# Pair loads, later weights, a new order of the scores and masks on another engine in a fused attention and mixing kernel

## The chip, the cores and the metric

One core of a Trainium2 chip. The metric is the device time of one execution in microseconds (us). Most executions of one kernel lie within a few us of one another. Engines are named as in the profile: PE (matrix products), DVE (vector), ACT (scalar), POOL (general purpose), SP (issues most of the DMAs).

A ratio between two kernels is the mean time of one kernel's fast runs over that of the other's in the same rounds. It is not quite the ratio of the medians quoted beside it.

## The reference

Eight batches, eight heads, 576 tokens, head size 64, all float32.

```python
q_d, k_d, v_d = mean of q, k, v over groups of 4 tokens           # 144 pooled tokens
out_up    = repeat(softmax(q_d @ k_d.T / 8) @ v_d, 4)             # pooled attention
out_local = softmax(q @ k.T / 8 where |i - j| < 4) @ v            # banded attention
x     = heads of (out_up + out_local) side by side                # (8, 576, 512)
theta = x @ w_theta
y     = w_tok_r @ (x * cos(theta)) + w_tok_i @ (x * sin(theta))   # over tokens
u     = x + y
out   = u + relu(u @ w_ch)
```

## The kernel before

Three generators make the work of a batch: `attention` (to x), `modulate` (theta, z) and `mix` (y and the output). A period runs attention of batch b+1, modulate of b and mix of b-1, interleaved by a fixed list. Attention 0 runs by itself, then the two token matrices are turned by PE, then the periods start. "First period" below is attention 1 with modulate 0; it has no mix. The parts that the change touches:

```python
TR = 96; NTR = S // TR                      # tokens of q, k in 6 tiles of 96
def load_qk(b):                             # 64 floats = 256 bytes in one piece
    for nm, src in (("q", q), ("k", k)):
        for c in range(6): nc.sync.dma_start(out=t[:, c, :, :],
            in_=src[b, :, TR*c:TR*c+TR, :].rearrange("h p d -> p h d"))
# [... load_v likewise; casts to bf16: batch 0 on DVE (q), POOL (k), ACT (v), later ones on POOL ...]
nc.gpsimd.dma_start(out=wth, in_=moe_w_theta ...)        # theta as bf16, software queue
for ri, w_dram in enumerate((moe_w_tok_r, moe_w_tok_i)): # token matrices, channel weights too
    nc.gpsimd.dma_start(out=t[:, 0:4, :], in_=w_dram[0:512, :] ...)
# [...]
def attention(b):
    # [... pstr: q, k turned and pooled by one product with ip = (identity | pooling);
    #      ACT copies the tokens to qT, kT, DVE the pooled ones to qdT, kdT; psvd: pooled v;
    #      psSd: pooled scores, exps on ACT to pd ...]
    for c in range(5):                                   # banded scores, exps, masks
        # [... psS products into a large PSUM tile, two of which exist (tag "w2") ...]
        nc.scalar.activation(out=pm[...], in_=ps[...], func=AF.Exp, scale=SCL)
        nc.gpsimd.affine_select(out=pm[...], in_=pm[...], ...)   # lower edge of the band
        nc.gpsimd.affine_select(out=pm[...], in_=pm[...], ...)   # upper edge
    for g in range(2):                                   # pooled output: psnd, also in "w2"
        # [... 16 products; rd = 1 / sum; xd = psnd * rd, both on DVE ...]
    for c in range(5):
        # [... psup (xd spread to tokens), psloc (pm @ v); rl, tmp, x on DVE ...]
# [... modulate, mix ...]
drain(attention(0)); drain(build_WT())                   # turning stands alone
for b in range(B + 1):
    run(attention(b + 1), modulate(b), mix(b - 1))       # with ends of the range cut
```

The softmax here doesn't subtract the row's maximum and nothing guards it: scores larger than these inputs give would overflow.

## Time and profile before

| | before |
|---|---|
| time of the runs beside the changed kernel | 360.19 us median of 4 (358.78 to 360.47) |
| profiled span, mean granted PE clock of the view | 358.8 us, 0.955 |
| last v cast of batch 0 ends | 38.48 us |
| last x of attention 0 ends | 56.24 us |
| first xTps (modulate 0 starts) | 62.29 us |
| psSd of batch 1 (pooled scores of the first period) | 75.49 us |
| first psth of the second period | 96.75 us |
| full periods at clock 1.0 | 36.06 us |

These landmarks are starts or ends of single instructions in the order of time. Two of them bracket the start of the program: up to the last v cast it waits for data, and from the first psth of the second period on every period looks alike. The prediction shows lines of the order of time (columns: start, duration, engine, source line, operation, output and inputs with sizes, count, and in brackets the idle time before it with what ended it).

```profile
86.48 0.69 DVE L319 TENSOR_TENSOR xd<-psnd,rd 72x512 bf16<-72x512 f32 x1
86.53 2.13 POOL L295 TENSOR_SCALAR_AFFINE_SELECT pm<-pm 128x1024 bf16<-128x1024 bf16 x2
...
88.52 0.69 DVE L355 TENSOR_TENSOR tmp<-psloc,rl 120x512 bf16<-120x512 f32 x1
...
92.94 0.87 POOL L298 TENSOR_SCALAR_AFFINE_SELECT pm<-pm 100x768 bf16<-100x768 bf16 x1
...
94.76 0.20 DVE L353 RECIPROCAL rl<-psloc 96x8 f32<-96x8 f32 x1 [1.18 <-PE psloc L346]
...
96.35 0.67 DVE L362 TENSOR_TENSOR x<-tmp,psup 96x512 bf16<-96x512 bf16 x1
```

POOL masks until 93.8. But DVE's rl, tmp and x start at 88.3 beside it and end at 97.0, and in these 8.7 us DVE waits only twice, 0.36 and 1.18 us.

A caution on the clock. A profile holds records of it only from its first rise on, at 67.2 us here and at 54.8 in the changed kernel, and the views count time without a record as 1.0. The products say otherwise. Two equal groups of the changed kernel, one before its first record and one after:

```profile
49.86 1.91 PE L484 MATMUL psth<-wth,xT 128*120 128x512 bf16 x4
...
55.18 1.03 PE L484 MATMUL psth<-wth,xT 128*120 128x512 bf16 x4
```

In all twenty profiles the products that turn q and k (pstr) follow one another every 120 ns (100 in the kernel before) both up to the first record and where half is recorded, and every 62 ns (52) where 1.0 is recorded. So up to the first record every kernel ran at half clock, and the clock that a view gives for a stretch ahead of the first record, or for one that reaches into it, is too high (the prediction's 0.73 over 62 to 96 us is some 0.65).

### The profile page before, as it was taken

The page shows a single profiled execution, that of the slowest core. Times are in us where ns is not written, and L with a number is a line of the kernel's source. Part 1 is how long each engine was busy: PE and PEld are TensorE (multiplying, and loading weights), DVE is VectorE, ACT ScalarE, POOL GpSimd, SP SyncE. Part 2 cuts the span into 40 slices and gives each one's busy share as a digit, 9 for nine tenths or more (in the row PEclk, how much of TensorE's full clock was granted, in tenths as well). Part 3 has the DMA queues.
Part 4 walks back from the last instruction along what each step waited for, and adds up shares of the span by engine and source line. Part 5 has one row for each costly group of instructions (what it writes and reads, how often), then busy time and mean ns, then how long its engine had stood idle before and what let it go on. Part 6 is the DMA issues. An engine that isn't in the chain of part 4 may idle for free.

```text
span 358.8 us, 7037 instructions
## 1 busy us (share of the span) xinstructions
PE 296.6 (83%) x2834; PEld 201.8 (56%) x2834; DVE 193.5 (54%) x435; ACT 192.1 (54%) x283; POOL 156.2 (44%) x153
## 2 busy tenths in 40 slices
PE   0025689948799989999899989998999899979995
PEld 0023368526566656665666666656665676657672
DVE  1121076533754494629574876287628752865433
ACT  1024802585267735782669366936693679334303
POOL 8011396308831783377147817583458003700000
PEclk9999999985589998999899999999999999999999
DMA  8999989990291069936994499766001200210303
GB/s 151 200 187 198 181 154 156 193 178 14 48 200 27 5 180 173 195 53 175 179 195 79 117 218 174 118 145 153 0 3 62 74 0 3 81 53 2 117 16 132
DMA packets 122577, 41.18 MB, mean 115 GB/s; under 512 B 115760, under 2 KB 117936, under 8 KB 122544
## 3 DMA queue, kind: packets, MB, share of 16 engines
q1 hardware_dynamic: 120272, 38.35, 55.2%
q0 software_dynamic: 2272, 2.38, 4.0%
q8 instruction: 22, 0.36, 0.4%
q14 instruction: 11, 0.09, 0.1%
HBM read 33.65 MB, written 9.44 MB: 120 GB/s over the span
## 4 chain that ended last, share of the span: by engine, by line
PE 47%; DVE 20%; ACT 15%; SPq 7%; issue 4%; POOL 3%; DMA 3%; POOLq 0%; ACTq 0%
PE psu L421 18%; PE psth L396 9%; SPq L80 6%; PE psr L439 6%; DVE osb L451 4%; DVE tmp L355 4%; DVE z L405 4%; DVE x L362 4%; PE pstr L212 3%; ACT pd L259 3%; PE psS L282 3%; ACT L259 2%; PE psnd L311 2%; PE wps L187 2%; ACT vd L240 2%
## 5 line engine op out<-in xcount | busy, mean ns | idle before, releaser
L421 PE MATMUL psu<-WT,z 120*128 120x288 bf16 (+1 forms) x640 | 93.6, 292 | 2.5 <-DVE uT L430 2.5
L421 PEld LDWEIGHTS <-z 120*128 120x128 bf16 (+1 forms) x640 | 60.5, 100 | 23.2 <-issue 3.6
L295 POOL TENSOR_SCALAR_AFFINE_SELECT pm<-pm 128x1024 bf16<-128x1024 bf16 (+1 forms) x40 | 41.2, 1047 | 65.5 <-ACT pm L289 65.5
L449 ACT ACTIVATE rel<-psr 128x512 f32<-128x512 f32 (+1 forms) x40 | 23.8, 596 | 61.7 <-PE psr L439 61.7
L430 DVE TENSOR_TENSOR uT<-psu,xT 128x288 bf16<-128x288 f32 x64 | 26.8, 452 | 50.7 <-PE psu L421 50.7
L396 PE MATMUL psth<-wth,xT 128*120 128x512 bf16 (+1 forms) x160 | 45.1, 406 | 7.6 <-DVE xT L386 6.8
L405 DVE TENSOR_TENSOR z<-cs,x 120x1024 bf16<-120x1024 bf16 (+1 forms) x40 | 39.1, 977 | 17.4 <-ACT cs L404 17.3
L219 ACT CAST qT<-pstr 128x576 bf16<-128x576 f32 x32 | 20.3, 640 | 52.1 <-PE pstr L212 52.1
L403 ACT ACTIVATE cs<-psth,pihc 120x512 bf16<-120x512 f32 (+1 forms) x40 | 27.5, 687 | 35.8 <-PE psth L396 35.6
L106 POOL CAST k_tm<-k 96x1536 bf16<-96x1536 f32 x16 | 24.5, 1547 | 41.6 <-DMA k<-in_k_dram 17.5
L439 PE MATMUL psr<-wch,uT 128*128 128x512 bf16 (+1 forms) x160 | 42.1, 379 | 0.0
L298 POOL TENSOR_SCALAR_AFFINE_SELECT pm<-pm 128x1024 bf16<-128x1024 bf16 (+1 forms) x40 | 41.1, 1047 | 0.3
L106 POOL CAST q_tm<-q 96x1536 bf16<-96x1536 f32 x14 | 23.2, 1679 | 40.5 <-PE pstr L212 32.2
L212 PE MATMUL pstr<-ip,q_tm 96*128 96x120 bf16 x192 | 19.8, 249 | 21.8 <-DVE ip L129 11.8
L289 ACT ACTIVATE pm<-psS 128x1024 bf16<-128x1024 f32 (+1 forms) x40 | 36.4, 981 | 1.9 <-PE psS L282 1.5
L451 DVE TENSOR_TENSOR osb<-rel,psx 128x512 f32<-128x512 f32 (+1 forms) x40 | 27.3, 682 | 7.9 <-ACT rel L449 7.1
L396 PEld LDWEIGHTS <-xT 128*120 128x120 bf16 (+1 forms) x160 | 20.5, 139 | 17.3 <-DVE xT L386 8.1
L212 PEld LDWEIGHTS <-q_tm 96*128 96x128 bf16 x192 | 14.6, 115 | 26.5 <-DVE ip L129 11.8
L386 DVE COPY xT<-xTps 128x480 bf16<-128x480 bf16 (+1 forms) x40 | 15.5, 389 | 25.7 <-PE xTps L381 25.6
L355 DVE TENSOR_TENSOR tmp<-psloc,rl 120x512 bf16<-120x512 f32 (+1 forms) x40 | 26.9, 685 | 0.1
L362 DVE TENSOR_TENSOR x<-tmp,psup 120x512 bf16<-120x512 bf16 (+1 forms) x40 | 26.5, 675 | 0.0
L346 PEld LDWEIGHTS <-pm 128*128 128x128 bf16 (+1 forms) x320 | 17.2, 113 | 15.9 <-issue 7.3
(68 smaller groups left out, 417.6 us busy)
## 6 DMA issues: line engine op xcount, KB each, us to landing
q<-in_q_dram SPq DMA_DIRECT2D x48, 192.0 KB, 5.6
k<-in_k_dram SPq DMA_DIRECT2D x48, 192.0 KB, 4.9
v<-in_v_dram SPq DMA_DIRECT2D x32, 256.0 KB, 5.3
out_dram<-osb SPq DMA_DIRECT2D x32, 256.0 KB, 2.0
v<-in_v_dram SPq DMA_DIRECT2D x8, 200.0 KB
out_dram<-osb SPq DMA_DIRECT2D x8, 128.0 KB
wtm<-in_moe_w_tok_r_dram POOLq DMA_DIRECT2D x1, 576.0 KB, 9.3
wtm<-in_moe_w_tok_i_dram POOLq DMA_DIRECT2D x1, 576.0 KB, 12.0
```

What stands on the lines that cost most here:

```text
L106: eng(out=dst[:, 3 * i:3 * i + 3], in_=src[:, 3 * i:3 * i + 3])
L212: nc.tensor.matmul(out=ps[:, c // 3, (c % 3) * TW:(c % 3) * TW + TW], lhsT=tm[:, c, 2 * hh:2 * hh + 2, :], rhs=ip, start=True, stop=True,)
L289: nc.scalar.activation(out=pm[0:kw, :, 0:qn], in_=ps[0:kw].rearrange("p e (j w) -> p (e j) w", w=P)[:, :, 0:qn], func=AF.Exp, scale=SCL,)
L295: nc.gpsimd.affine_select(out=pm[0:kw, :, 0:qn], in_=pm[0:kw, :, 0:qn], compare_op=ALU.is_ge, fill=0.0, base=off, pattern=[[0, 8], [-1, qn ...
L298: nc.gpsimd.affine_select(out=pm[0:kw, :, 0:qn], in_=pm[0:kw, :, 0:qn], compare_op=ALU.is_ge, fill=0.0, base=6 - off, pattern=[[0, 8], [1, ...
L355: nc.vector.tensor_tensor(out=tmp[0:cnt].rearrange("p (j e d) -> p e j d", e=2, j=4), in0=pv[0:cnt, :, :, 0:D], in1=rl[0:cnt].unsqueeze(3) ...
L362: nc.vector.tensor_tensor(out=x[0:cnt], in0=tmp[0:cnt], in1=up[0:cnt], op=ALU.add)
L396: nc.tensor.matmul(out=th[0:cnt, :], lhsT=xT[:, dc, QS[c]:QS[c] + cnt], rhs=wth[:, dc, :], start=(dc == 0), stop=(dc == 3),)
L405: nc.vector.tensor_tensor(out=z[0:cnt, c, :, :], in0=cs[0:cnt], in1=xt[c][0:cnt].unsqueeze(1).to_broadcast([cnt, 2, DM]), op=ALU.mult,)
L421: nc.tensor.matmul(out=pss[hf][:, 0:288], lhsT=z[0:QC[c], c, ri, P * dc:P * dc + P], rhs=WT[0:QC[c], ri, c, 288 * hf:288 * hf + 288], star ...
L439: nc.tensor.matmul(out=psr[0:cnt, :], lhsT=uT[:, dc, OS[c]:OS[c] + cnt], rhs=wch[:, dc, :], start=(dc == 0), stop=(dc == 3),)
L451: nc.vector.tensor_tensor(out=osb[0:cnt], in0=rel[0:cnt], in1=psx[0:cnt, 0:DM], op=ALU.add)
```

## The change

The intent: the start waits for data, and DMA is full there with pieces of 256 bytes. So q and k are loaded as pairs of tokens (512 bytes), q by head. Theta comes as float32 by the hardware queue, the other weights are asked for inside the first period, and the turning of the token matrices goes into that period too. POOL's masks at the start move to DVE as one product with a band. The pooled output moves ahead of most banded scores. The pair layout costs an interleaving write on ACT. Two small savings: five psvd products instead of six, and the last output block as 128 x 256 instead of 64 x 512.

```diff
-                        in_=src[b, :, TR * c:TR * c + TR, :].rearrange("h p d -> p h d"),
+                        in_=src[b, h].rearrange("(c p r) d -> p c (r d)", c=NTR, r=2),        # q, by head
+                    in_=src[b, :, TB * c:TB * c + TB, :].rearrange("h (p r) d -> p h (r d)", r=2),   # k
-    nc.gpsimd.dma_start(out=wth, in_=moe_w_theta.rearrange("(c p) e -> p c e", p=P))
+    nc.sync.dma_start(out=w32, in_=moe_w_theta.rearrange("(c p) e -> p c e", p=P))   # cast by POOL
-    w_tm = [] ... nc.gpsimd.dma_start(...)          # token matrices, wch outside
     def build_WT():
+        w_tm = [] ... nc.gpsimd.dma_start(...)      # now inside
-                    in_=pv[:, :, :, 0:TR],
+                    out=To[:, hh, :].rearrange("p (c w r) -> p c r w", c=NTR, r=2),   # ACT, interleaving
-        for g, cs in ((0, (0, 1, 2)), (1, (2, 3, 4))):
+        for g, cs in ((0, (0, 1, 2)), (1, (3, 4))):
+            if b == 0 or (b == 1 and c % 2 == 0):
+                nc.vector.tensor_tensor(out=pv, in0=pv, in1=band[min(c, 1)]..., op=ALU.mult)
+            else: nc.gpsimd.affine_select(...) twice, as before
-        for c in range(NCH): scores; then for g in range(2): pooled output
+        scores(0); pooled_out(0); scores(1); pooled_out(1); scores(2); scores(3); scores(4)
-    drain(build_WT())
-            mix(b - 1) if b >= 1 else None)
+            mix(b - 1) if b >= 1 else build_WT())
# [... cut: constants, casts in thirds with a pace, last output block, buffers of v_w and vd kept ...]
```

## The prediction

> **What bounds the kernel now.** I read the row of slices first, then a table of busy time by stage, then the order of time of the first 65 us, then the chain that ended last inside one full period, then the groups and the DMA queues.
>
> ```profile
> PE   0025689948799989999899989998999899979995
> POOL 8011396308831783377147817583458003700000
> PEclk9999999985589998999899999999999999999999
> DMA  8999989990291069936994499766001200210303
> ```
>
> A slice is 9 us. The DMA engines are full for the first nine slices while PE is empty for two and partly filled until slice 10; POOL is full where PE's clock falls (slices 8 to 10). From slice 11 on PE is at 9 tenths. So there is a start of some 96 us that PE does not bound, and a steady part that PE nearly does. The table by stage gives sizes (columns: window, length, busy us and count on PE, PEld, DVE, ACT, POOL, granted clock, DMA share, GB/s):
>
> ```profile
> 12.00:30.00 18.00, 3.48 (x30) 2.57 (x27) 2.19 (x5) 2.42 (x4) 2.91 (x2) 1.00 1.09 194
> 54.00:62.00 8.00, 8.00 (x56) 6.40 (x54) 5.67 (x13) 2.56 (x3) 5.74 (x6) 1.00 1.04 157
> 62.00:96.20 34.20, 24.92 (x234) 17.22 (x233) 17.22 (x41) 18.33 (x28) 17.17 (x16) 0.73 0.65 105
> 135.00:172.70 37.70, 35.20 (x348) 23.45 (x348) 23.13 (x53) 23.70 (x36) 19.30 (x17) 0.95 0.73 150
> 210.60:246.60 36.00, 33.51 (x348) 22.55 (x348) 23.20 (x53) 23.68 (x36) 21.38 (x18) 1.00 0.85 164
> ```
>
> The first 30 us hold 4 us of PE work: attention of batch 0 waits for data. 54 to 62 is the turning of the two token matrices, alone. 62 to 96 is the first overlapped period, without mix, yet as long as a full one. Full periods last 36.0 at full clock, up to 38.8 where it drops.
>
> The order of time shows the waits of the start:
>
> ```profile
> 10.66 0.96 DVE L106 CAST q_tm<-q 96x1536 bf16<-96x1536 f32 x1 [8.00 <-DMA q<-in_q_dram]
> 19.46 0.96 DVE L106 CAST q_tm<-q 96x1536 bf16<-96x1536 f32 x1 [7.74 <-DMA q<-in_q_dram]
> 28.55 1.46 POOL L106 CAST k_tm<-k 96x1536 bf16<-96x1536 f32 x1 [1.76 <-DMA k<-in_k_dram]
> 37.87 0.61 ACT L111 CAST v_w<-v 100x512 bf16<-100x512 f32 x1
> 43.62 2.13 POOL L298 TENSOR_SCALAR_AFFINE_SELECT pm<-pm 128x1024 bf16<-128x1024 bf16 x2
> 56.16 0.81 DVE L192 COPY WT<-wps 120x576 bf16<-120x576 bf16 x2
> 62.29 0.98 PE L381 MATMUL xTps<-ident,x 120*128 120x120 bf16 x8
> ```
>
> q is complete at 19.5, k at 28.6, v at 37.9; then POOL masks five score blocks, two passes of 1.07 each, to 53; then the turning; modulate of batch 0 begins at 62.3. In the period after it the chain is
>
> ```profile
> 81.27 1.03 ACT pm L289
> 82.36 2.13 POOL pm L295 x2
> 84.50 2.09 POOL pm L298 x2
> 86.58 2.09 POOL pm L295 x2
> ```
>
> POOL to 93.8, with PE idle and its clock halved. In a full period (135 to 173) the chain is PE to the second psr, then some 10 us of DVE (osb, tmp, x in turn) to the next xT. The DMA side:
>
> ```profile
> q1 hardware_dynamic: 120272, 38.35, 55.2%
> q0 software_dynamic: 2272, 2.38, 4.0%
> ```
>
> **What the Trainium skill says.** "DMA: Bandwidth & Descriptors", section Specifications, puts the least transfer for full rate at 512 B; its section on small descriptors adds a fixed overhead per packet. The trace agrees in kind: 115760 of 122577 packets are under 512 B and saturated stretches move 154 to 200 GB/s. "TensorE: Matmul & The Clock Gate", Part 1, says that an idle window of about 3.4 us halves the clock: the trace has 0.73 over 62 to 96. "VectorE: DVE Perf Modes", tier table, gives tensor_tensor on bf16 in SBUF two elements a cycle; the like-shaped z product takes 0.68 us undisturbed (0.93 on average), so a mask product should cost 0.65 to 0.95 instead of POOL's 2 x 1.09. "TensorE", Part 3, says that products with outputs in different column groups run side by side; no row of this trace shows that yet.
>
> **The change, part by part.**
>
> *DMA.* The hardware queue took 0.552 x 16 x 358.8 = 3169 us of engine time for 120272 packets. Taking 75 ns for each of the 4608 output packets of 2 KB (estimate from 27 GB/s per engine, the page's Specifications), the 256 B ones take 24.4 ns. For 512 B I add 256 B at that rate, 9.4 ns: 34 ns, an estimate. Per batch, over 16 engines: q or k 4608 x 24.4 = 7.0 us before, 2304 x 34 = 4.9 after; v 4896 x 24.4 = 7.5 in both. The software queue's weights took 4.0% = 14.4 us: each token matrix 3.8, each square one 3.4; theta as float32 on the hardware queue 512 x 75 = 2.4. The busy share stood near 1.1 when saturated, so I divide sums by 1.1 and start at 2 us.
>
> The instruction order shows a catch: the first token matrix's load is not a period later at all; it is POOL's first instruction. The second and the channel weights do wait, behind v's casts. So: first token matrix and q0 land at 2 + 8.7/1.1 = 10, k0 at 14.4, v0 at 21.2; then theta, second token matrix, channel weights and q1 (14.5) at 34, k1 at 39, v1 at 46.
>
> *Attention 0.* q cast 12; but the pooling half of ip is behind the first k cast on POOL (13). Four q groups took 3.6 us, so 16.6. PE then meets a psvd product between the first and second k group, which needs v's first cast; POOL does 4.6 us of constants first, so that cast ends near 21. k groups to 25, last v cast 25, pooled exps 26 to 28.7, five banded exps of 0.98 to 34, masks on DVE right behind. DVE then has five tmp, x and rl of 1.5 each: first x at 36, last at 41.5. So modulate 0 starts at 36 against 62.3: 26 us gained, 12 from data that comes earlier, 7 from the masks, and the rest from the turning that no longer stands alone.
>
> *First period.* In before, xTps to vd took 14.3 us (ACT and PE mixed), so vd at 51.5 with 1 us for q copies that were done ahead before; inputs are there (v1 at 46, cast 48). Table load and pooled exps to 57, banded exps to 62. Three of five masks are on DVE; blocks 1 and 3 stay on POOL, behind casts of batch 2 (q2 50, k2 55, v2's first part 58), so they end near 61 and 65. x done 67, first psth 67 against 96.95: the period takes 31 to 32 instead of 34.7, though it holds the turning (50 products, 5.9 to 8 us PE; 4.5 us DVE), since POOL's 11 us of masks are gone from its chain. Gain so far 30.
>
> *Full periods.* psvd is five products of 512 columns instead of six: -0.21. The last output block is 128 x 256 instead of 64 x 512: DVE 0.67 to about 0.4, ACT 0.59 to 0.38, PE 0 to -0.4. The pooled product and its rd/xd go ahead of the scores, but PE's sum ahead of the second psr stays and the chain did not wait for xd. POOL casts 9 pieces of about 1.03 instead of 7 (+0.4), off the path. So -0.5 a period, six periods -3; the last two stages -0.5 each. Total 360.3 - 30 - 3 - 1 = 326.
>
> **Rivals.** (1) *Transfers hidden anyway:* if the start were bound by latency and not by DMA time, loads by pairs would give little. Against: share 0.98 to 1.28 until 54 us, and waits on q and k stand at the head of three casts. It would leave only masks and turning, some 343. (2) *POOL or v take the wait's place:* psvd early in PE's order, and casts of batch 2 ahead of batch 1's masks, make v0 and v2 the gate. I count part of it; if SWDGE packets crowd out q0 as they did at 6 to 23 us, where the second half of q took 9 us longer than the first, all slips by 5 to 8: 332 to 334. (3) *Strided ACT writes:* q and k are written two elements apart now; if 0.64 became 1.1, ACT gains 4 us a period and a period might lengthen by 1 to 2: 335. ACT's 24 us of 36 speak for slack. (4) *Clock:* three boundaries in before lost 1.7 each; the shorter period may meet the idle windows none or five times: +-5.
>
> **Range and chances.** Lengths of the start are good to 5 us each way, the clock to 5, the periods to 3: 317 to 336. For less than 2% (above 353) the whole start would have to fail. Faster 0.97, same 0.02, slower 0.01.
>
> **What would show it.** q_tm casts near 10, last k cast near 15, last v cast near 25; first xTps near 36; first period's POOL masks ending near 65; psth of the second period near 67; full periods of 35.3 to 35.6 at clock 1.0; relu and osb of the last block near 0.4. Wrong would be: q landing after 14, qT copies over 0.7, a PE wait on v_w of several us beyond 21, or periods no shorter than 36.

## The result

| | before | after | predicted |
|---|---|---|---|
| time, median of 4 | 360.19 us | 346.18 us (342.45 to 347.6) | 326 (317 to 336) |
| ratio of fast runs | 1 | 0.9584, 95% interval 0.9503 to 0.9666 | |
| last v cast of batch 0 ends | 38.48 | 28.76 | 25 |
| last x of attention 0 ends | 56.24 | 50.01 | 41.5 |
| first xTps | 62.29 | 45.92 | 36 |
| psSd of batch 1 (the prediction is for vd, which began at 76.50 and 63.28) | 75.49 | 62.16 | 51.5 |
| first psth of the second period | 96.75 | 85.75 | 67 |
| from there to the last period's first psth | 221.4 | 218.5 | about 218.4 |
| from there to the end | 40.7 | 41.7 | about 39.7 |

The changed kernel is faster by some 4%, and 20 us slower than predicted, outside the range. The profiled execution was the slowest of its four (347.6, marked slow for being 1.5% above the fastest); every reading below is repeated in fast profiles of the experiments. Rows of its page and its hardware queue:

```profile
PE   0148889898999889998999899979998999889994
PEclk9999999755899989998999999999999999989999
DMA  8989989967089374618354564520003000300303
...
q1 hardware_dynamic: 84448, 39.40, 47.3%
```

A slice is 8.6 us. PE fills up two slices earlier than before, and DMA's full stretch is shorter: the queue took 47.3% instead of 55.2%. But PE's clock still falls, in slices 7 to 10 (up to 54.8 us, in slice 6, it has no record and was at half), and the boundary that stood at slice 11 has only moved to slice 10. The order of time of the start:

```profile
13.15 1.89 DVE L134 CAST q_tm<-q 96x1024 bf16<-96x1024 f32 x3 [9.53 <-DMA k<-in_k_dram]
...
18.96 1.03 POOL L134 CAST k_tm<-k 96x1024 bf16<-96x1024 f32 x1 [1.05 <-DMA k<-in_k_dram]
...
25.19 0.58 PE L297 MATMUL psvd<-v_w,pu 128*90 128x512 bf16 x1 [3.88 <-POOL v_w L137]
...
28.14 0.62 POOL L141 CAST v_w<-v 100x512 bf16<-100x512 f32 x1
...
36.60 1.17 PE L384 MATMUL psnd<-vd,pd 90*72 90x65 bf16 x16 [0.92 <-DVE xd L392]
36.85 1.53 DVE L363 TENSOR_TENSOR pm<-pm,band 128x1024 bf16<-128x1024 bf16 x1 [0.30 <-POOL q_tm L134]
...
45.92 0.56 PE L469 MATMUL xTps<-ident,x 120*128 120x120 bf16 x4
```

(The releaser named for the q cast is the load that landed last by the profile.) q and k are complete at 15 and 20 instead of 20.4 and 30, v at 28.8 instead of 38.5. PE stands 3.9 us for v's first cast, which POOL makes behind 4 us of constants. A pooled output waits for DVE, and a mask takes 1.53 us where 0.65 to 0.95 was expected. The table by stage, first for the first period and then for two full ones (columns as in the prediction's table):

```profile
45.92:85.75 39.83, 36.03 (x305) 24.84 (x304) 27.64 (x60) 23.12 (x32) 18.60 (x17) 0.74 0.95 196
85.75:122.89 37.14, 34.75 (x350) 23.67 (x352) 22.30 (x51) 25.00 (x36) 22.16 (x21) 0.96 0.57 138
197.42:233.02 35.60, 33.11 (x349) 22.83 (x351) 21.86 (x51) 24.64 (x36) 20.12 (x19) 1.00 0.52 132
```

The first period got longer: 39.83 from first xTps to the next first psth, against 34.46. PE is busy for 36 of it, at a clock of 0.74 by the view, or some 0.63 if the 8.9 us without a record count as half. Full periods at clock 1.0 are 35.60, as predicted. So all of the shortfall lies ahead of 85.75 us, but for the tail, which lost 1.0 instead of gaining 1 (a fall of the clock, see below). The last output block came as foreseen: its osb 410 ns and its relu 384. And its products in two column groups do run side by side, as the prediction expected: the two of a pair start 3 to 30 ns apart, and pair follows pair after 0.11 us.

### The profile page after: what moved, and what is told of

Its sections match the earlier page's. It is cut to its first block, busy times and chain, and to the rows that moved or that the text cites. A ratio compares the mean times of both kernels' runs of the same rounds, so it can differ in the third digit from the quotient of the medians.

```text
span 345.9 us, 7082 instructions
## 1 busy us (share of the span) xinstructions
PE 296.1 (86%) x2844; PEld 203.2 (59%) x2858; DVE 193.0 (56%) x440; ACT 198.1 (57%) x280; POOL 152.5 (44%) x162
## 3 DMA queue, kind: packets, MB, share of 16 engines
q1 hardware_dynamic: 84448, 39.40, 47.3%
## 4 chain that ended last, share of the span: by engine, by line
PE 47%; DVE 19%; ACT 19%; issue 5%; DMA 4%; SPq 3%; POOL 2%; ACTq 0%; DVEq 0%
PE psu L509 17%; PE psth L484 12%; DVE tmp L442 5%; DVE x L449 5%; PE pstr L272 5%; DVE osb L556 4%; PE psnd L384 4%; ACT pm L357 3%; ACT pd L323 3%; DMA k<-in_k_dram 2%; ACT L323 2%; ACT cs L491 2%; ACT rel L554 2%; PE psr L529 2%; PE psS L349 2%
## 5 line engine op out<-in xcount | busy, mean ns | idle before, releaser
L509 PE MATMUL psu<-WT,z 120*128 120x288 bf16 (+1 forms) x640 | 91.3, 291 | 0.0
L370 POOL TENSOR_SCALAR_AFFINE_SELECT pm<-pm 128x1024 bf16<-128x1024 bf16 (+1 forms) x32 | 33.8, 1064 | 48.8 <-ACT pm L357 48.8
L357 ACT ACTIVATE pm<-psS 128x1024 bf16<-128x1024 f32 (+1 forms) x40 | 38.5, 982 | 20.7 <-PE psS L349 14.2
L554 ACT ACTIVATE rel<-psr 128x512 f32<-128x512 f32 (+1 forms) x40 | 22.4, 559 | 48.0 <-PE psr L529 37.7
L280 ACT CAST qT<-pstr 128x576 bf16<-128x576 f32 x32 | 25.5, 802 | 42.1 <-PE pstr L272 42.1
L134 POOL CAST q_tm<-q 96x1024 bf16<-96x1024 f32 x21 | 27.0, 1321 | 47.9 <-PE pstr L272 38.1
L134 POOL CAST k_tm<-k 96x1024 bf16<-96x1024 f32 x24 | 27.6, 1176 | 41.9 <-DMA k<-in_k_dram 16.2
L493 DVE TENSOR_TENSOR z<-cs,x 120x1024 bf16<-120x1024 bf16 (+1 forms) x40 | 31.4, 786 | 17.5 <-ACT cs L492 17.5
L491 ACT ACTIVATE cs<-psth,pihc 120x512 bf16<-120x512 f32 (+1 forms) x40 | 27.5, 688 | 23.8 <-PE psth L484 23.4
L272 PE MATMUL pstr<-ip,q_tm 96*128 96x144 bf16 x192 | 21.5, 264 | 18.4 <-POOL ip L161 16.2
L372 POOL TENSOR_SCALAR_AFFINE_SELECT pm<-pm 128x1024 bf16<-128x1024 bf16 (+1 forms) x32 | 33.4, 1053 | 1.0
L529 PE MATMUL psr<-wch,uT 128*128 128x512 bf16 x114 | 31.3, 379 | 1.4 <-issue 0.8
L272 PEld LDWEIGHTS <-q_tm 96*128 96x128 bf16 x192 | 17.1, 116 | 23.0 <-DVE ip L163 16.0
L484 PEld LDWEIGHTS <-xT 128*120 128x120 bf16 (+1 forms) x160 | 20.4, 141 | 16.0 <-DVE xT L474 6.8
L280 ACT CAST kT<-pstr 128x576 bf16<-128x576 f32 x32 | 24.9, 809 | 6.4 <-PE pstr L272 6.4
L449 DVE TENSOR_TENSOR x<-tmp,psup 120x512 bf16<-120x512 bf16 (+1 forms) x40 | 26.8, 681 | 0.0
```

The lines of the kernel that those rows point to most:

```text
L134: eng(out=dst[:, c].rearrange("p r h d -> p h r d"), in_=src[:, c].rearrange("p h (r d) -> p h r d", r=2))
L272: nc.tensor.matmul(out=ps[:, c, TR * r:TR * r + TR + TP], lhsT=tm[:, c, r, 2 * hh:2 * hh + 2, :], rhs=ip[:, TR * r:TR * r + TR + TP], star ...
L280: nc.scalar.copy(out=To[:, hh, :].rearrange("p (c w r) -> p c r w", c=NTR, r=2), in_=bass.AP(tensor=parts.tensor, offset=parts.offset, ap= ...
L357: nc.scalar.activation(out=pv, in_=ps[0:kw].rearrange("p e (j w) -> p (e j) w", w=P)[:, :, 0:qn], func=AF.Exp, scale=SCL,)
L370: nc.gpsimd.affine_select(out=pv, in_=pv, compare_op=ALU.is_ge, fill=0.0, base=off, pattern=[[0, 8], [-1, qn]], channel_multiplier=1)
L449: nc.vector.tensor_tensor(out=x[0:cnt], in0=tmp[0:cnt], in1=up[0:cnt], op=ALU.add)
```

## The experiments

All edits are against the changed kernel unless said otherwise. Eighteen kernels ran; all gave a result that passed the comparison. The runs of one group shared a chip and the runs of the kernel before (median 360.64, 359.02, 359.01, 360.32 and 359.36 us in the five groups, in the order of this section save where noted). Landmarks in us from each profile:

| run | time, median (range) | ratio to before | last v cast | first xTps | psSd of batch 1 | second period's first psth | full period at clock 1.0 |
|---|---|---|---|---|---|---|---|
| e1_scores_first | 342.34 (341.82 to 343.96) | 0.9526 | 26.79 | 44.97 | 60.62 | 83.30 | 35.42 |
| e2_masks_pool | 347.44 (346.0 to 349.17) | 0.9662 | 27.65 | 43.77 | 66.35 | 87.40 | 35.59 |
| e3_both | 343.24 (342.96 to 343.63) | 0.9544 | 27.43 | 42.94 | 61.98 | 83.41 | 35.42 |
| e4_turn_alone | 349.93 (347.57 to 351.86) | 0.9720 | 27.35 | 55.70 | 67.50 | 89.14 | 35.60 |
| e7_const_first | 340.42 (338.24 to 344.15) | 0.9515 | 25.16 | 40.72 | 55.41 | 78.72 | 35.59 |
| e8_late | 336.81 (333.04 to 336.98) | 0.9417 | 20.08 | 34.90 | 50.71 | 74.07 | 35.59 |
| e10_hold_casts | 341.87 (340.83 to 342.28) | 0.9580 | 27.99 | 44.26 | 59.15 | 81.70 | 35.41 |
| e11_warm | 346.75 (345.89 to 348.13) | 0.9725 | 26.97 | 44.25 | 63.16 | 85.37 | 35.59 |
| e9_loads_alone | 351.04 (350.37 to 352.14) | 0.9805 | 29.29 | 58.23 | 72.05 | 92.32 | 35.42 |
| c3_first_late_hold | 332.85 (329.65 to 335.0) | 0.9264 | 20.33 | 34.84 | 50.52 | 73.20 | 35.42 |
| c4_fill | 333.23 (332.83 to 333.97) | 0.9311 | 20.37 | 35.92 | 52.06 | 72.73 | 35.42 |
| e12_fill | 343.56 (342.16 to 344.33) | 0.9588 | 28.16 | 45.46 | 60.97 | 83.20 | 35.60 |
| e6_weights_start | 345.30 (344.71 to 346.17) | 0.9598 | 28.25 | 45.59 | 62.18 | 84.56 | 35.59 |
| e15_contig | 343.11 (339.92 to 343.61) | 0.9506 | 27.45 | 44.46 | 59.41 | 82.08 | 35.47 |
| e13_wt_act | 334.79 (330.3 to 335.09) | 0.9275 | 19.98 | 35.66 | 53.64 | 76.39 | 35.42 |
| e14_masks1_pool | 334.45 (333.11 to 338.16) | 0.9283 | 20.30 | 35.29 | 51.79 | 75.64 | 35.42 |
| c7_first_late | 334.76 (330.78 to 336.11) | 0.9294 | 20.64 | 35.64 | 51.99 | 75.24 | 35.41 |
| c8_first_late_fill | 332.94 (331.46 to 334.32) | 0.9274 | 20.94 | 35.39 | 50.78 | 72.22 | 35.41 |

Two cautions. In kernels that do not touch the loads the last v cast moves between 26.8 and 28.8 from profile to profile. And one to three of the six full periods lose some 1.65 us to the clock in each profile (the first of them up to 3.0, as the half clock of the first period reaches into it). So a time difference below 2 us says little, and lengths between landmarks say more. The profiles of e14 and c7 fell in slow runs. Ratios compare within a group only: the fast runs of the kernel before averaged 356.5 and 356.7 us in the first two groups and 358.1 to 359.9 in the others.

### Order, masks and turning (one group)

e1 puts the five score blocks ahead of the two pooled outputs again. e2 puts all masks back on POOL. e3 does both. e4 turns the token matrices ahead of the first period.

```diff
# e1
-        scores(0); pooled_out(0); scores(1); pooled_out(1); scores(2), (3), (4)
+        scores(0), (1), (2), (3), (4); pooled_out(0); pooled_out(1)
# e2
-            if b == 0 or (b == 1 and c % 2 == 0):
+            if False:
# e4
     drain(attention(0))
+    drain(build_WT())
-            mix(b - 1) if b >= 1 else build_WT())
+            mix(b - 1) if b >= 1 else None)
```

> The changed kernel with the five banded score blocks ahead of the two pooled outputs, as in the kernel before; masks on DVE stay. In the changed kernel the five exps of batch 0 run from 33.9 to about 42, one per 2 us, last x of attention 0 at 50.0, first xTps 45.9, second period's first psth 85.75, 346.2 us. Theory A (the new order paces the exps through the two large PSUM buffers and DVE): exps back to back again, 33.9 to 39.2; last x 46 to 47; first period 2 to 4 us shorter or earlier, second period's first psth 81 to 83; 342 to 343.5 us. Rival B (DVE's tail of tmp and x, or POOL's casts, would have filled the gap anyway): exps to 39, but last x 49 to 50, second period's first psth 85 to 86, 345 to 347 us. Full periods unchanged in both.

> The changed kernel with every mask back on POOL, order as changed. If the masks on DVE are worth what the prediction took for them (7 us in attention 0, and POOL's 11 us off the chain of the first period): last x 52 to 54, second period's first psth 91 to 95, 352 to 356 us. Rival (the paced order hides the masks wherever they run, since an exp comes only every 2 us and two POOL passes take 2.15): last x 51 to 52, second period's first psth 87 to 88, 347 to 349 us.

> Scores first and masks on POOL: order and mask engine as before, loads, weights and turning as changed. If each part is worth something by itself: second period's first psth 90 to 95, 352 to 355 us. If the two parts of the change cancel one another (new order costs what the DVE masks save): exps to 39, masks on POOL 35 to 46, last x about 50, second period's first psth 85 to 87, 345 to 348 us.

> The changed kernel with the token matrices turned after attention of batch 0 and ahead of the first period, as in the kernel before. Theory A (inside the first period PE runs at half clock and is on the path, so that the 50 transposes cost there what they cost alone): first xTps 52 to 54, first period (first xTps to next first psth) from 39.8 down to 33 to 35, second period's first psth 85 to 88, time 345 to 348 us. Rival B (turning inside the period is hidden, as predicted): first period 38 to 40, second period's first psth 92 to 94, time 352 to 354 us.

*Order.* With scores first the five exps run back to back (31.9 to 36.3), and the time is 342.34, as theory A said; but its landmarks did not follow: the last x ended at 49.06, rival B's figure, and the second period began at 83.30, just outside theory A's 81 to 83. Between e2 and e3, which differ in the order alone and shared a chip, the time is 4.2 us apart and the ranges do not meet. Part of that is in the steady part, which I had not expected: full periods are 35.42 with scores first and 35.60 with the pooled output ahead, 0.18 times six. That this part of the change costs time is shown by the pair e2 and e3, and in direction by e1.

*Masks.* They are worth little in either order: e2 to the changed kernel 347.44 to 346.18, e3 to e1 343.24 to 342.34. Yet the masks on DVE did what was predicted of them within attention 0: with masks on POOL the last x ends at 58.4 (e2) against 50.0, and at 54.5 (e3) against 49.1. The second period's first psth moves by 1.7 and by 0.1 only (by 2.8 and by -0.5 if both are counted from the last v cast). Modulate and attention 1 start with the first x, so the gain of 5 to 8 us fell off the path. The prediction for e2 (352 to 356) failed, and so did its rival's landmark for the last x, though the rival's time held. e3 met neither of its forecasts: 343.24 us where 345 to 348 was the lower, with the last x at 54.5 and not about 50.

Why the masks took longer than expected on DVE is in e1's order of time:

```profile
33.00 0.69 DVE L363 TENSOR_TENSOR pm<-pm,band 128x1024 bf16<-128x1024 bf16 x1 [5.21 <-ACT pm L357]
...
33.84 3.92 POOL L134 CAST q_tm<-q 96x1024 bf16<-96x1024 f32 x3 [4.85 <-DVE pm L363]
...
33.91 5.70 DVE L363 TENSOR_TENSOR pm<-pm,band 128x1024 bf16<-128x1024 bf16 x4 [0.22 <-ACT pm L357]
```

The mask that ran alone took 0.69 us. The four that ran while POOL cast q took 5.70 together, and POOL's three casts 3.92 instead of 3 times 1.04. This is tested below (e10).

*Turning.* Alone it takes PE 5.87 us for 35 of its transposes:

```profile
49.89 5.87 PE L241 MATMUL wps<-ident,wtm 128*120 128x128 bf16 x35
```

First xTps moves from 45.9 to 55.7 and the period behind it falls from 39.8 to 33.4 us, as theory A said. But not all of these 6.4 us are the turning: in e4 every x is there when the period starts, so that first psth follows first xTps after 1.08 us instead of 3.94. From first psth to the next it is 32.37 against 35.89 in the changed kernel and 33.7 to 35.2 in like ones (e6, e7, e8, e15), so the turning inside the period costs 1.3 to 3.5 us. The time is 3.8 us above the changed kernel (separate rounds; 7.6 above e1 of the same rounds, which differs in the order too), and attention 0's last products then no longer overlap with modulate 0 (4.1 us from first xTps to last x in the changed kernel). Theory A had the period right and the total wrong (345 to 348 foreseen); the move was worth some 4 us, not the 7 that the prediction's sum leaves for it.

### Constants, weights, casts and the clock (second group)

```diff
# e7: pooling matrices, bands and ru written ahead of the k casts
# e8: token matrices and wch held until v of batch 0 is cast
+            nc.gpsimd.tensor_copy(out=t[0:1, 0:5, 0:1], in_=v_ws[0][0:1, 4, 0:5, 0:1])
             nc.gpsimd.dma_start(out=t[:, 0:4, :], in_=w_dram[0:512, :] ...)      # same for wch
# e10: e1, and POOL's casts of batch 1 held until the last mask of batch 0
+            nc.gpsimd.tensor_copy(out=q_tm[0:1, 0, 0, 0, 0:1], in_=pms[-1][0:1, 0, 0:1])
# e11: four products of 128 x 512 on constants ahead of each turning step
+            for _ in range(4): nc.tensor.matmul(out=ps, lhsT=ident, rhs=wm, start=True, stop=True)
```

> The changed kernel with POOL's constants (pooling matrices, bands, ru: some 4 us) ahead of its k casts instead of between the last k cast and the first v cast. If they hold the start up (PE stood 3.9 us for the first v cast in the changed kernel): first v cast 20 to 22 instead of 24.1, last v cast 25 to 26 instead of 28.8, everything after it 2 to 3 us earlier, second period's first psth 83, 343 to 344 us. Rival (v's bytes land late anyway, so casts wait for DMA in their place): v casts within 1 us of the changed kernel, 345 to 347 us. Arrival of q and k varies by 1 to 1.5 us from run to run, so lengths from the last k cast on are what is compared.

> The changed kernel with both token matrices and the channel weights held until the last v piece of batch 0 is cast (a tiny POOL copy from that piece into each destination), so that the first token matrix no longer loads beside q and k; the scheduler then also sets the constants ahead of the k casts. If the first token matrix's load delays q and k: it is 3.8 us of all 16 engines, so last k cast 15.5 to 17.5 instead of 18 to 19, last v cast 23 to 25, second period's first psth 80 to 83, 341 to 344 us. Rival (q and k land as late without it): last k cast as before within 1 us, 344 to 347 us; and if turning comes to wait for its matrices, the first period gets longer by 1 to 3 us.

> Scores first (as the earlier run of that name), and POOL's casts of batch 1 held until the last mask of batch 0 is done. In the run with scores first the first mask on DVE took 0.69 us alone and the other four 5.70 us together while POOL cast q. Theory A (POOL's casts slow DVE's masks): masks 0.69 each, all done one to 1.5 us behind the last exp, last x 3 us earlier measured from the first exp (16.5 to 13.5 us); then 339 to 341 us if batch 1's inputs come in time. Rival B (the masks are slow by themselves): masks stay near 1.4 and the time rises by 0 to 3 us. Rival C (casts then hold the first period's q group): last x earlier but first psth of the second period unchanged, 342 to 344 us.

> The changed kernel with 52 products of 128 x 512 on constants, results unused, four ahead of each turning step of the first period: some 11 us more of PE work at full clock, in a period whose PE work is some 19 us at full clock. Theory A (the half clock from 64 to 88 us, not the amount of work, sets this period): the clock stays at 1.0 for most of it, products take half the time, and the second period's first psth comes 2 to 5 us earlier, 342 to 344 us. Rival B (waits on ACT and DVE set it and the half clock costs nothing): clock higher, but psth unchanged within 1 us, 345 to 347 us. Rival C (the clock falls all the same): the extra products cost 8 to 20 us.

*e7* gave more than expected: the last v cast at 25.16 as foreseen, and 340.42 us instead of 343 to 344. From the last v cast to the second period's first psth it needs 53.6 us instead of 57.0. Why that stretch became shorter as well I did not separate.

*e8* is the largest single gain, 336.81 us where 341 to 344 was foreseen. Its casts:

```profile
7.97 1.29 DVE L134 CAST q_tm<-q 96x1024 bf16<-96x1024 f32 x2 [4.34 <-DMA q<-in_q_dram]
...
13.94 1.04 POOL L134 CAST k_tm<-k 96x1024 bf16<-96x1024 f32 x1
...
19.46 0.62 POOL L141 CAST v_w<-v 100x512 bf16<-100x512 f32 x1 [0.39 <-DMA v<-in_v_dram]
```

q at 8 instead of 13, the last k cast done at 15 instead of 20, the last v cast at 20.1 instead of 28.8. In the changed kernel the first token matrix is asked for inside the generator of the first period, but its load depends on nothing, so the build put it at the head of POOL's queue. "A period later" was true of the source and not of the program. e8 also has the constants early; set against e7, the held loads by themselves are worth 5.1 us of data and 3.6 us of time.

*e10* shows theory A on the masks:

```profile
34.20 0.69 DVE L367 TENSOR_TENSOR pm<-pm,band 128x1024 bf16<-128x1024 bf16 x1 [5.19 <-ACT pm L361]
35.11 1.53 DVE L367 TENSOR_TENSOR pm<-pm,band 128x1024 bf16<-128x1024 bf16 x2 [0.22 <-ACT pm L361]
36.86 1.25 DVE L367 TENSOR_TENSOR pm<-pm,band 128x1024 bf16<-128x1024 bf16 x2 [0.22 <-ACT pm L361]
```

With POOL quiet every mask takes about 0.7 (the five 3.5 us together, against 6.4 in e1). The Trainium skill, "SBUF — State Buffer", section "SBUF: two separate sides", says that DVE and POOL share one pair of ports, that a DVE operation with two inputs in SBUF (a mask is one) competes for it with a POOL operation that reads SBUF, and that the loser is blocked for the whole instruction; the pair 0.69 and 1.43 agrees, and so does the line of e11 below. From first exp to last x it took 15.3 us instead of 17.2, but the time did not move (341.87 against 342.34). So this gain too falls mostly off the path; that is rival C's outcome in time.

*e11* kept the clock at full from 52.1 us on and won nothing. A line of DVE, with the POOL cast beside it:

```profile
62.15 3.01 POOL L134 CAST k_tm<-k 96x1024 bf16<-96x1024 f32 x3 [4.73 <-issue]
...
62.89 2.81 DVE L505 TENSOR_TENSOR z<-cs,x 96x1024 bf16<-96x1024 bf16 x1 [1.24 <-ACT cs L504]
```

The first period was 41.1 us. The added products stand on its chain of waits for some 10 us, so this run could not say what the half clock costs. The lines show the shared ports at their worst: a z product of 0.68 us took 2.81 beside three k casts.

### The loads alone, the gains together, a smaller filler (third group)

```diff
# e9: loads by pairs, everything else back: e1 + e2 + e4, theta as bf16 and all weights outside build_WT
# c3: e8 + e1 + the held casts of e10
# e12: two products ahead of each pooled and banded score block of batch 1, into the same PSUM tile
+            if b == 1:
+                for _ in range(2): nc.tensor.matmul(out=ps[:, 0, :], lhsT=ident, rhs=wm, start=True, stop=True)
# c4: c3 with those products for batches 0 and 1
```

> The changed kernel with everything but the loads put back: scores first, all masks on POOL, turning ahead of the first period, theta by the software queue as bf16 and all weights asked for outside the turning, as in the kernel before. What remains is the pair loads with their products, the five psvd products and the last output block of 256 columns. Sum of single effects measured so far: changed 346, scores first -4, turning alone +4, masks on POOL +1, weights at the start +0 to +2: 347 to 350 us, last v cast 29 to 31, full periods of 35.4 at clock 1.0. If the loads alone gave less than that, because the other parts are what let them through: 352 to 356 us.

> Token matrices and channel weights held until v of batch 0 is cast, scores first, and POOL's casts of batch 1 held until the last mask: three single gains together. If they add (late 9.5, order 4, hold 0.5 of the changed kernel's 346): 331 to 334 us, last v cast 20, last x 34 to 36, second period's first psth 68 to 70, full periods 35.4. If they overlap (the first period then waits for batch 1's casts or for the token matrices, which now come after masks): 335 to 338 us, first period over 40.

> The run before it with two extra products of 128 x 512 (constants, overwritten by the real ones) ahead of each block of pooled and banded scores of batches 0 and 1, 32 in all, placed where PE waits for ACT's exps. In the run that holds the token matrices the clock was half from 23.7 to 43.6 and again from 57.7. Theory A (the half clock follows from short gaps there, and costs PE time that is on the path): clock near 1.0 over both stretches, second period's first psth 3 to 7 us earlier, time 3 to 7 us below the run before it. Rival B (clock held, but ACT and DVE set the time): clock near 1.0, time within 1.5 us. Rival C (gaps too long for 16 products a batch): clock still half, time 1 to 3 us more.

> The changed kernel with the same two extra products ahead of the score blocks of batch 1 only (16 products, 3.5 us at full clock) in place of the 52 of the earlier run, which held the clock at 1.0 but put some 9 us of themselves on the path and left the first period at 41. Theory A (half clock makes 5 to 8 us of the 39.8): clock over 0.9 from 62 to 86, first period 33 to 36, second period's first psth 79 to 82, 340 to 343 us. Rival B (clock held, period unchanged): first period 38.5 to 40. Rival C (clock falls all the same): first period 40 to 43, 347 to 350 us.

*e9*, 351.04 us: the loads by pairs and the small savings make 8 of the 14 us. The last v cast is at 29.3, as early as in the whole change. So the change's own handling of weights brought the data no further. The sum of single effects had said 347 to 350, a little too low.

*c3* is 332.85 us, the gains added as theory A said, though the second period began at 73.2 and not at 68 to 70; the first did not go over 40 (38.4). *c4* kept the clock up in much of both stretches, made the first period 1.6 us shorter and attention 0 about a microsecond longer, and ended equal: 333.23 (rival B's time).

*e12* held the clock at 1.0 from 52.5 to 76 us with a third of e11's products; up to 52.5, and from 76.4 to 86.6, it was half. The first period took 37.7 instead of 39.8, the time 343.56. That lies between A (33 to 36) and B. Profiles of like kernels without the filler (the changed one, e6, e7, e8, e15) spread from 37.6 to 39.8, so the half clock that the filler took away cost some 2 us at most here, not the 8 that were missing. In attention 0, c4 had full clock from 23.1 to 36.8 where c3 had half, and gained nothing; what half clock costs from first xTps to 52.5 no run tells.

### What bounds the first period (fourth and fifth group)

```diff
# e6: theta as bf16 and all weights asked for outside build_WT, as in the kernel before
# e15: ACT writes q and k without interleaving tokens; wrong tokens on purpose
-                    out=To[:, hh, :].rearrange("p (c w r) -> p c r w", c=NTR, r=2),
+                    out=To[:, hh, :].rearrange("p (c r w) -> p c r w", c=NTR, r=2),
# e13: c3 with WT's second half copied by ACT
+                (nc.scalar.copy if ri else nc.vector.tensor_copy)(out=WT[...], in_=ps[...])
# e14: c3 with the masks of batch 1 on POOL
-            if b == 0 or (b == 1 and c % 2 == 0):
+            if b == 0:
# c7: c3 without the held casts.   c8: c7 with the filler of e12
```

> The changed kernel with theta as bf16 by the software queue at the very start and all other weights asked for outside the turning, as in the kernel before. POOL's queue then starts with theta and the first token matrix. If the weights part of the change is worth what it should be (theta out of the way of q and k, 3.4 us of all DMA engines): q, k and v 2 to 4 us later, last v cast 30 to 33, 348 to 351 us. If it brought little, since the first token matrix still loads at the start in both: last v cast within 1.5 us of the changed kernel's 27 to 29, 345 to 348 us.

> The changed kernel with ACT's copies of q and k written without the interleave of tokens, so that writes are contiguous; the result is wrong on purpose. Copies should fall from 0.80 to 0.64 us. If the strided writes cost time: full periods at clock 1.0 shorter than 35.60 by 0.5 to 1.3 us (8 copies of 0.16), 339 to 343 us. If ACT's slack holds them: full periods 35.5 to 35.6, first period and attention 0 at most 0.5 us shorter each, 345 to 346.5 us.

> The version with the token matrices held, scores first and casts held (332.9 us), with the second half of the turning's copies (5 of 0.45 us) on ACT, which is idle at the end of the first period where DVE is full. If DVE is the bound of that end: first period (psth to psth) from 34.4 to 32.2 to 33.4, 331 to 332 us. If PE at half clock is: 34.2 to 34.6 and 332.5 to 333.5 us. If ACT's exps come later for it: 34.5 to 35.5.

> The same version with batch 1's masks all on POOL, so that only batch 0's are on DVE. If DVE is the bound of the first period: three masks of 0.9 to 1.4 off it, first period 34.4 to 32 to 33.5. If POOL's masks, behind its casts, become the gate instead (two passes of 1.09 each for five blocks, after casts of batch 2): first period 36 to 38, 334 to 337 us. If neither, since masks lie in a gap of DVE: within 0.5 us.

> The changed kernel with scores first and with token matrices and channel weights held until v of batch 0 is cast; POOL's casts of batch 1 run freely. If the hold of casts brought its 2 us of DVE masks: 334 to 336 us. If the hold only moves the wait to the first period's q group: 331 to 333 us, first xTps to first psth 3.9 to 4.1 us as without the hold. Full periods 35.4 at clock 1.0.

> The same with two extra products ahead of each score block of batch 1 (16 in all). If the half clock costs the first period 2 us or more: psth to psth 1.5 to 3 us shorter than in c7, 1 to 3 us less in time. If DVE's chain of xd, tmp and x sets it whatever the clock: clock near 1.0 from 56 to 68 us, time within 1 us of c7.

*e6*: 345.30, last v cast 28.3. The weights part of the change, as it was built, brought nothing that can be measured.

*e15*: the copies fell from 0.802 to 0.640 us, as this group of it shows:

```profile
L280 ACT CAST qT<-pstr 128x576 bf16<-128x576 f32 x32 | 20.5, 640 | 44.3 <-PE pstr L272 44.2
```

Full periods became 0.13 shorter (35.47), so ACT's slack holds the strided writes there. The time was 343.11, below the 345 to 346.5 foreseen for that case; its profile has the data 1.3 us earlier than the changed kernel's and a first period of 37.6, and 1 to 2 us of the start may be the copies' own. The comparison passed although the tokens are wrong: q and k are of size 0.1, so scores are near 0.01 and the softmax is nearly even. That test does not guard this part of the kernel.

*e13* and *e14* took work off DVE in the first period, and neither made it shorter (40.7 and 40.4 us against 38.4 for c3; times 334.79 and 334.45). The expectation that DVE's extra work bounds it failed twice. In both, psSd of batch 1 also came later, so the runs do not price that work finely.

*c7* and *c8*: the filler made the first period 36.8 instead of 39.6 us and the time 332.94 instead of 334.76, with ranges that overlap. The stretch from psSd to the next period is still 21.4 us, although the clock was full to about 69 us. The table by stage of c8 there:

```profile
62.00:66.00 4.00, 2.57 (x37) 1.87 (x36) 3.76 (x10) 0.00 (x0) 3.65 (x4) 1.00 0.89 225
66.00:70.00 4.00, 3.09 (x35) 2.08 (x33) 4.00 (x11) 0.00 (x0) 2.13 (x3) 0.91 1.02 250
```

PE waits, ACT does nothing, and DVE is full: rd, xd and five times rl, tmp and x, in one row, with a mask and copies of WT between them. In the changed kernel the same row, from the first rl on, has no gap at all:

```profile
77.39:85.38 7.99, 6.91 (x59) 4.86 (x58) 7.99 (x18) 0.80 (x1) 1.77 (x2) 0.50 0.85 159
```

No experiment brought the stretch from psSd on below 20.3 us. Holding the casts (c3 against c7) is worth at most 2 us, and the ranges overlap.

c3 and c8 are the best versions: 332.85 and 332.94 us, ratios 0.9264 and 0.9274. Dividing these by 0.9584 gives 3.3% and 3.2% below the changed kernel, from separate rounds.

## Why the prediction was wrong

Its sum was 30 for the start, 3 for the periods, 1 for the end. The periods were right: 35.60 at clock 1.0 where 35.3 to 35.6 was said, 2.9 us in all. The end lost 1.0 to the clock: the changed kernel's record has it at half from 304.0 to 307.4, at the first psth of the last period, and in the three profiles without a fall there (e2, e3, c3) the end took 40.1 us, so at full clock it gained 0.6. The start gave 11. From the prediction's own landmarks the missing 18.75 us of the start split so:

| stretch | predicted | measured | miss |
|---|---|---|---|
| to the last v cast | 25 | 28.76 | 3.8 |
| last v cast to first xTps | 11 | 17.16 | 6.2 |
| first xTps to batch 1's pooled scores | 15.5 | 16.24 | 0.7 |
| from there to the second period | 15.5 | 23.59 | 8.1 |

The prediction's 51.5 is for vd and not for psSd. Counted to vd (63.28), the last two misses are 1.9 and 7.0. (Two of its readings were a little off too: its 96.95 is 96.75, and 27 in the skill's Specifications is in GiB/s.)

**Data (3.8).** The packet estimate held. The packed trace has the time of every packet: those of 512 bytes took 35.3 ns on average where 34 was taken, those of 256 bytes 20.9 (23.8 in the kernel before; 24.4 taken), and output packets of 2 KB 87 where 75 was taken. The prediction even noted that the first token matrix loads first, and charged it 3.8 us of engine time, 3.5 at a share of 1.1. Counted by these packets (the last one of each), q had landed at 10.6 (10 said), k at 17.7 (14.4) and v at 23.8 (21.2); in e8, with that load held, at 6.8, 12.3 and 18.4. So the charge was right for q (3.8), but k and v lost 5.3 and 5.4 to it (4.5 and 4.7 with e7, of the same rounds, in place of the changed kernel). The step that failed here is the charge of its bytes alone: 1.0 to 1.9 of the 3.8 us. The wait for POOL's constants was in the sum (PE's wait for the first v cast was put at 16.6 to 21 and took 3.9), but POOL's row behind v's landing, with the issues of the other weights between the casts, took 5.0 and not 3.8. Why k and v lose more than the load's bytes stays open. Rival 2 had said that such packets may crowd out the others, and was given 332 to 334.

**Attention 0 behind v (6.2).** The prediction had exps back to back to 34 and the first x two us behind. The new order paced the exps (ACT waited 0.84, 1.60 and 0.92 us between them; e1), masks beside POOL's casts took up to twice their time (e10), and rd and xd stood ahead of tmp in DVE's row. First exp to first x took 10.0 us instead of 7.3; with scores first it was no shorter (e1: 10.7), only the waits changed place. The masks' 7 us were real at the last x (e2: 58.4 against 50.0) and worth 1 to 2 in the end, because the next period hangs on the first x and on batch 1's inputs.

**The end of the first period (8.1).** This is the step that failed most: "POOL's 11 us of masks are gone from its chain". In all nineteen profiles of changed kernels the stretch from psSd of batch 1 to the second period's first psth lies between 20.3 and 23.9 us, with masks on DVE or POOL, either order, and clock high or low; before it was 21.26. With all masks of batch 1 on POOL it was 21.1 and 21.4 (e2, e3), with three on DVE 23.6 and 22.7 (the changed kernel, e1); e14 against c3 goes the other way, 23.9 to 22.7. The chain of waits named POOL because POOL was the last to release each step. The prediction also read PE as idle there, but from 81 to 97 us of the kernel before PE was busy for 12.4 of 16, at half clock. And DVE's rd, xd, rl, tmp and x ran beside POOL with 1.5 us of waits in 8.7 (the lines shown of before). Taking POOL away left the exps in a row on ACT, then DVE's row, full for 8 us in the changed kernel. After the last banded exp I allowed 5 us; in c8, at high clock, it ended at 61.2 and the second period began at 72.2, so 11 were needed. Half clock is part of it, some 2 us (psSd to psth 21.4 in c8 against 23.3 in c7, whose profile was slow, and 20.7 in c4 against 22.7 in c3, both fast). That removing POOL's masks shortens the stretch by 1.2 us at most is shown; that DVE's row is what bounds it is read from the lines and not shown by a run: e13 and e14 took other work off DVE without gain, and none shortened the row itself.

**The turning.** The text expected it hidden, since the period has idle PE. It costs 1.3 to 3.5 us inside the period (e4). The 4 us that the move won are about the 4.1 by which modulate 0 now overlaps with the end of attention 0. The prediction counted this overlap, and then took lengths from a profile in which all x were done before the period began; first xTps to first psth was 1.08 us there and 3.94 now, as DVE still made x. From first xTps to the first clock record (45.9 to 54.8) PE was also busy for 8.35 of 8.88 us at half clock; no run changed that, and what it costs is open.

**Rivals.** Transfers hidden anyway (343) is refuted by the data's 9.7 us, although its number was nearest. ACT's strided writes (335) cost 0.13 us a period, not 1 to 2. The clock as a swing of 5 covers the falls at boundaries, some 1.65 us each, one to three in every profile and at times one in the end; it does not cover the half clock inside the first period, some 2 us.

By parts, in time: the pair loads 8 us (e9), the turning some 4 (e4), the masks about 1 (e2, e1 and e3), the weights nothing as built (e6), and the new order cost up to 4 (e2 and e3). These come from different rounds and need not add exactly.

## What to carry to other kernels

A chain of waits names the engine that let go last; before you credit the removal of its work, look at what the other engines do in the same microseconds, because a nearly full row beside it may become the bound at once. Look up where a built program places a load, not where the source asks for it: what depends on nothing starts first, and may take the DMA from what the start waits for. And ask of every early finish which instruction waits for it: five to eight us at the last x were worth almost nothing, since the next stage hung on the first x.

## What the Trainium skill lacked or had wrong

- No page says that a profile's clock record can begin late and that a mean over it then counts the start as full. Here it begins at 67.2 us (before) and 54.8 (changed), with pstr products every 100 and 120 ns up to there and every 52 and 62 at recorded full clock. By these lengths "TensorE: Matmul & The Clock Gate", Part 4, is right that transposes do not count as busy for the clock: in the kernel before, PE ran transposes alone from 56.5 to 63.3 us without a gap, and the clock rose only at 67.2, behind theta's products.
- The table of the same page, Part 1, has the clock halve after an idle window of about 3.4 us; short idles between groups come later in that part, without a size. Here no such window was idle. In the 3.4 us ahead of the fall PE was busy for 0.47 of the time in the kernel before (77.4 us), 0.75 in the changed one (65.0) and 0.79 in e1 (66.3), with no gap over 1.22, 0.54 and 0.45 us. In e8 it stayed at half from 23.3 to 43.8 us with PE mostly above 0.85 busy, and came back only when PE had been without a gap from 39 us on. Short gaps were enough to lose it and to keep it lost.
- "SBUF — State Buffer", section "Door 1: The DMA port swizzle", says that bf16 accesses may stride by up to 8 elements for free. ACT's copies to every second bf16 element took 0.802 us for 128 x 576 and 0.640 us when contiguous (e15).
- The section "SBUF: two separate sides" of that page is right on the ports that DVE and POOL share, but gives no size for a product of two inputs beside a cast: masks 0.69 us alone and 1.43 beside casts (e1), and one z product 2.81 instead of 0.68 (e11).
- No page has it that a DMA asked for late in the source is issued at the head of its queue by the build when nothing holds it; that cost up to 5 us of data here (e8 against e7).
